# Retention attention and a bilinear feed-forward on one core: other zero products, 64x128 state updates and a new order in the first two pairs

## Chip, cores, metric

One core of one Trainium2 chip. The metric is device time in microseconds (us) of one execution of the program; the times given are medians over several runs.

## The reference

A retention layer (4 batches, 8 heads, 768 steps, head width 64) is followed by a bilinear feed-forward network with 512 inputs and 1536 hidden columns. All inputs and the result are float32.

```python
gamma = 1.0 - 2.0 ** (-5.0 - np.arange(H))
for t in range(S):
    state = gamma * state + einsum('bhd,bhe->bhde', k[:, :, t], v[:, :, t])
    y[:, :, t] = (1 / sqrt(D)) * einsum('bhd,bhde->bhe', q[:, :, t], state)
x = y.transpose(0, 2, 1, 3).reshape(B * S, H * D)      # 3072 x 512
out = ((x @ w_a) * (x @ w_b)) @ w_out                  # 512 -> 1536 -> 512
```

The kernel computes the retention in chunks. With powers of gamma folded into q and k ("scalings", two tables `ktab` and `qtab`), a chunk's result is masked scores times v (within the chunk) plus q times the running state (from the chunks before).

## The kernel before

The 3072 rows are 24 slots of 128 rows. The first six slots (the first batch) are handled as three pairs: a pair is 256 rows, of which slot `par` (0 or 1) holds the even or the odd ones, and a pair has two chunks c of 128 rows each. All other slots take another path (`casts`, `turn`, `scores`, `inter`, `intra`), which the change does not touch. Feed-forward work is cut into eight row tiles J of 512 or 256 rows; tile 0 is the rows of pairs 0 and 1.

Order is written out by hand. Every engine instruction goes through `seq`, which chains it to the one before on its engine, so the order in the source is the order on each engine; semaphores between engines are added by the framework from the tiles that instructions share. There is no planner.

The steps of a pair u, with their names:

- `casts2` (L376) scales k and q into bf16 (`scaled`, L212) and casts v (L184), each on the engine that is named: `D_` is DVE (VectorE), `G_` is POOL (GpSimd), `A_` is ACT (ScalarE).
- `flip2` (L387) transposes k or q on PE (TensorE, L396) into PSUM and copies the result to SBUF (`kT2`, `qT2`).
- `scores2` (L399) makes one slot's scores as 16 products in 64x64 quarters of the PE array (L409); `mask2` (L415) multiplies them with the causal mask on DVE, as two instructions (r = 0, 1).
- `update2` (L422) adds a chunk's k-v products to the state in PSUM (L432), as 16 products in 64x64 quarters; `keep_state` (L439) copies the state's two diagonal halves to `gbd` in SBUF with two ACT instructions.
- `intra2` (L454) multiplies masked scores with v (32 products per pair, L461), `inter2` (L443) adds queries times the kept state (L449). Both write `y`, a PSUM bank for each chunk; `leave2` (L466) copies `y` to `xt`, the input of the feed-forward, one instruction for a chunk.
- `warm` (L481) issues products with a tile of zeros (L484). They compute nothing that is used and keep PE busy.

The state makes pair 0 and pair 1 a chain: an update of chunk c, its copy to `gbd`, the next update into the same bank, and so on; `inter2` of a chunk needs the copy made after the chunk before.

The feed-forward: `ffn_a` (L497) is four products for x @ w_a of 128 hidden columns and an ACT copy of the result, `ffn_g` (L510) four products for x @ w_b and a DVE multiplication with that copy, `ffn_out` (L535) the last product. For tile 0 and the first two groups of hidden columns (ft 0 and 1) the rows are split in two halves: the first half are the rows of pair 0, the second those of pair 1. `parts` (L491) splits the rows for ft 2 and 3 as well, into two products of 256 columns within one instruction group. Pair 2 is worked on between the groups of tile 0.

PSUM has eight banks here: three rotating ones (`psff`, tag "ff"), `y0`, `y1`, the two banks of `at`, and one for the state (`st`).

Loads are DMAs on SyncE's queue in the order of `LOADS`: k and q of pair 0, k and q of pair 1, v of both, and then the weights, which POOL casts to bf16 (`cast_w`, `cast_o`). The first ten are issued at the start. POOL works in the order of the source, too.

Of the kernel before, what the change touches and what calls it, by code (L numbers as in the profile page):

```python
# [9 lines left out]
F32 = mybir.dt.float32  # L10
BF16 = mybir.dt.bfloat16
# [12 lines left out]
def kernel(  # L24
# [10 lines left out]
    nc = tc.nc  # L35
# [86 lines left out]

    kqb = {}
    issue_loads(10)
    zero = const.tile([P, 2 * P], BF16, name="zero")
    seq(nc.vector.memset(zero, 0.0))  # L126
    lgr = const.tile([P, 1, H], F32, name="lgr")
    bq = const.tile([P, 1], F32, name="bq")
# [106 lines left out]
    def half(i):  # L235
        return slice(64 * i, 64 * i + 64)
# [139 lines left out]
    def casts2(u, on):  # L376
        if 2 * u not in kqb:
            for t in (2 * u, 2 * u + 1):
                new_nat(t)
        for (i, par), eng in on.items():  # L380
            t = 2 * u + par
            if i == V:
                cast(eng, vb[t], raws["v", t])
            else:
                scaled(eng, t, i)

    def flip2(u, i, on, banks=None):  # L387
        into = (kT2, qT2)[i]
        if u not in into:
            into[u] = tra.tile([P, 2, HP, P], BF16, tag="kq"[i] + "T2", name="kq"[i] + "T2", bufs=2)  # L390
        for pars, eng in on:
            pool, tag = (psff, "ff") if banks is None else (psat, banks[pars[0]])
            tp = pool.tile([P, 2, HP, P], BF16, tag=tag, name="tp")[:, : len(pars)]
            for m, par in enumerate(pars):
                for hp in range(HP):
                    seq(nc.tensor.transpose(tp[:, m, hp, :], kqb[2 * u + par][:, i, hp, :, :], ident))  # L396
            cast(eng, into[u][:, pars[0] : pars[0] + len(pars)], tp)

    def scores2(u, par, ff=False):  # L399
        t = 2 * u + par  # L400
        if not ff:
            both = psat.tile([P, 2, HP, P], F32, tag="at", name="at")
            at = [both[:, r] for r in range(2)]
        else:
            at = [psff.tile([P, HP, P], F32, tag="ff", name=f"at{r}") for r in range(2)]
        for hp in range(HP):
            for c in range(2):
                for r in range(2):
                    seq(nc.tensor.matmul(at[r][half(c), hp, :],  # L409
                                         kT2[u][half(r), par, hp, half(c)],  # L410
                                         qT2[u][half(r), :, hp, half(c)],
                                         start=True, stop=True, skip_group_check=True))
        ats[t] = at

    def mask2(u, par):  # L415
        t = 2 * u + par
        aT[t] = tra.tile([P, 2, HP, P], BF16, tag="aT", name="aT")
        for r in range(2):
            seq(nc.vector.tensor_tensor(aT[t][:, r], ats[t][r], masks[par].to_broadcast([P, HP, P]),  # L419
                                        op=ALU.mult))  # L420

    def update2(u, c, keep=True):  # L422
        if (u, c) == (PAIRS - 1, 1):
            return
        if (u, c) == (0, 0):
            state[0] = psst.tile([P, HP, D], F32, tag="st", name="st")
        st = state[0]
        for par in range(2):
            for hp in range(HP):
                for r in range(2):  # L430
                    t = 2 * u + par
                    seq(nc.tensor.matmul(st[half(r), hp, :], kb[t][half(c), hp, r, :],  # L432
                                         vb[t][half(c), HP * r + hp, :],
                                         start=((u, c, hp, par) == (0, 0, 0, 0)),
                                         stop=(hp == HP - 1), skip_group_check=True))
        if keep:
            keep_state(c)

    def keep_state(c):  # L439
        for r in range(2):  # L440
            seq(nc.scalar.copy(gbd[1 - c][half(r), :, half(r)], state[0][half(r), :, :]))

    def inter2(u, last=False):  # L443
        for c in range(2):
# [9 lines left out]
    def intra2(u, par, begin, home=(psat, "y0", "y1")):  # L454
        if begin:
            ys[u] = [home[0].tile([P, HP, P], F32, tag=home[1 + c], name="y") for c in range(2)]
        t = 2 * u + par
        for r in range(2):
            for hp in range(HP):
                for c in range(2):  # L460
                    seq(nc.tensor.matmul(ys[u][c][half(hp % 2), 2 * r + hp // 2, :],  # L461
                                         vb[t][half(c), HP * r + hp, :], aT[t][half(c), r, hp, :],
                                         start=(begin and r == 0 and hp < 2), stop=not begin,
                                         skip_group_check=True))
# [11 lines left out]
    def xcols(J, kt, c0, c1):  # L476
        if J < 2:
            return xt[J][:, c0 // P : c1 // P, kt, :]
        return xt[J][:, kt, c0:c1]

    def warm(n, pool, tag, w=2 * P):  # L481
        idle = pool.tile([P, 4 * P], F32, tag=tag, name="idle")
        for _ in range(n):
            seq(nc.tensor.matmul(idle[:, :w], zero[:, :P], zero[:, :w], start=True, stop=True,  # L484
                                 skip_group_check=True))
# [2 lines left out]

    asbs = {}

    def parts(J, ft, c0, c1):  # L491

        if J == 0 and ft in (2, 3):
            return [(c0, (c0 + c1) // 2), ((c0 + c1) // 2, c1)]
        return [(c0, c1)]

    def ffn_a(J, ft, c0=0, c1=None):  # L497
        c1 = TILES[J] * P if c1 is None else c1
        if J not in ht:
            ht[J] = htp.tile([P, NFT, 4 * P], BF16, tag="ht", name="ht")  # L500
        fs = slice(ft * P, (ft + 1) * P)
        a = psff.tile([P, 4 * P], F32, tag="ff", name="a")[:, : c1 - c0]
        for kt in range(KT):
            for b0, b1 in parts(J, ft, c0, c1):
                seq(nc.tensor.matmul(a[:, b0 - c0 : b1 - c0], wa_bf[:, kt, fs], xcols(J, kt, b0, b1),  # L505
                                     start=(kt == 0 and b0 == c0), stop=(kt == KT - 1 and b1 == c1),
                                     skip_group_check=True))
        asb = asbs[J, ft, c0] = asbp.tile([P, 4 * P], BF16, tag="asb", name="asb")[:, : c1 - c0]
        seq(nc.scalar.copy(asb, a))  # L509

    def ffn_g(J, ft, c0=0, c1=None):
        c1 = TILES[J] * P if c1 is None else c1
        fs = slice(ft * P, (ft + 1) * P)
        g = psff.tile([P, 4 * P], F32, tag="ff", name="g")[:, : c1 - c0]
        for kt in range(KT):
            for b0, b1 in parts(J, ft, c0, c1):
                seq(nc.tensor.matmul(g[:, b0 - c0 : b1 - c0], wb_bf[:, kt, fs], xcols(J, kt, b0, b1),  # L517
                                     start=(kt == 0 and b0 == c0), stop=(kt == KT - 1 and b1 == c1),
                                     skip_group_check=True))
# [88 lines left out]
    for ft in range(2, NFT):  # L608
# [9 lines left out]
            ffn_g(0, ft + 1)  # L618
        if ft == 8:
            ffn_ab(0, ft)  # L620
    flip2(2, K, [((0, 1), A_)], ("y0",))
    ffn_a(0, 9)
    flip2(2, Q, [((0,), D_), ((1,), D_)], ("y1", "y0"))
    ffn_g(0, 9)
# [80 lines left out]
```

## Time and profile before

| | |
|---|---|
| median of 3 runs | 226.02 us (225.84 to 283.55) |
| the profiled execution | 226.63 us |
| its span, first to last instruction | 224.9 us |
| PE busy | 218.5 us (97%), 2632 products |
| DVE, ACT, POOL busy | 96.3 us, 96.3 us, 80.4 us |
| moved by DMA | 39.72 MB |

How to read the profile: times are us from the start of the span. PE's products are pipelined, so a product's row lasts longer than the distance to the next one; what a product costs in a stream is the distance between starts. "Timeline" rows give the start, the time to the end of the last of a group, engine, source line, output<-inputs, tile shapes and count; in brackets stands how long the engine was idle before, and who ended it. "Waits" rows give who waited for whom, the total, the count and the longest.

### The profile page before, as it was taken

The numbers are of one execution on the slowest core, as the hardware profiler recorded it, in microseconds if no ns is written. First come the engines' busy times: TensorE is split into PE (matmuls) and PEld (weight loads), VectorE is DVE, ScalarE is ACT, GpSimd is POOL, SyncE is SP. The second block draws the span as 40 slices with busy tenths as digits, with TensorE's granted clock in tenths as the row PEclk, the third lists the DMA queues.
The fourth block names the chain that finished last, engine by engine and source line by source line (L and its number), as shares of the span: only waits on it lengthen the run. The fifth ranks groups of instructions, "written<-read, shape, count | busy, mean of one in ns | idle before, by whom it ended". The sixth has DMA issues, their size and how long they took to land.

```text
span 224.9 us, 6284 instructions
## 1 busy us (share of the span) xinstructions
PE 218.5 (97%) x2632; PEld 133.5 (59%) x2632; DVE 96.3 (43%) x195; ACT 96.3 (43%) x207; POOL 80.4 (36%) x105
## 2 busy tenths in 40 slices
PE   8879999999999999999999999999999999999994
PEld 8768645686456866876875444554444544444443
DVE  3784347553406435472466333544343521334300
ACT  3475435433427426454457333355333354333221
POOL 5577798682544335350533535251000000000000
PEclk9999999999999999999999999999999999999999
DMA  6999999899999994988958899895100012100022
GB/s 179 347 379 383 365 314 407 260 206 194 228 243 271 222 223 80 223 222 186 212 135 194 127 226 239 187 235 146 47 0 0 3 50 93 47 3 1 0 93 95
DMA packets 96124, 39.72 MB, mean 177 GB/s; under 512 B 76000, under 2 KB 91616, under 8 KB 96096
## 3 DMA queue, kind: packets, MB, share of 16 engines
q1 hardware_dynamic: 95952, 39.20, 67.8%
q8 instruction: 20, 0.33, 0.6%
q10 hardware_dynamic: 144, 0.13, 0.2%
q14 instruction: 8, 0.07, 0.1%
HBM read 28.31 MB, written 6.29 MB: 154 GB/s over the span
## 4 chain that ended last, share of the span: by engine, by line
PE 96%; DVE 1%; issue 1%; ACT 0%
PE o L545 28%; PE a L505 28%; PE g L517 28%; PE idle L484 3%; PE y L321 1%; PE at L280 1%; PE y L333 1%; PE tp L396 1%; PE st L257 1%; PE y L449 1%; PE st L432 1%; DVE aT L419 1%; DVE kqb L212 1%; PE y L461 0%; PE at L409 0%
## 5 line engine op out<-in xcount | busy, mean ns | idle before, releaser
L520 DVE TENSOR_TENSOR ht<-g,asb 128x256 bf16<-128x256 f32 (+1 forms) x98 | 53.9, 550 | 84.2 <-PE g L517 74.3
L505 PE MATMUL a<-xt,wa_bf 128*128 128x256 bf16 (+1 forms) x400 | 77.6, 319 | 0.0
L517 PE MATMUL g<-xt,wb_bf 128*128 128x256 bf16 (+1 forms) x400 | 77.6, 319 | 0.0
L509 ACT CAST asb<-a 128x256 bf16<-128x256 f32 (+1 forms) x98 | 46.3, 473 | 71.2 <-PE a L505 71.2
L545 PE MATMUL o<-wo_bf,ht 128*128 128x512 bf16 (+2 forms) x312 | 64.4, 363 | 0.0
L505 PEld LDWEIGHTS <-wa_bf 128*128 128x128 bf16 x400 | 38.8, 98 | 24.0 <-DVE xt L184 0.4
L517 PEld LDWEIGHTS <-wb_bf 128*128 128x128 bf16 x400 | 39.0, 98 | 23.0
L545 PEld LDWEIGHTS <-ht 128*128 128x128 bf16 x312 | 28.8, 98 | 30.5
L212 POOL TENSOR_TENSOR kqb<-kf,ktab 128x512 bf16<-128x512 f32 x22 | 22.9, 1044 | 40.5 <-DMA kf<-in_k_dram 35.9
L182 ACT COPY osb<-o 128x512 f32<-128x512 f32 (+2 forms) x25 | 14.1, 565 | 32.9 <-PE o L545 27.6
L184 POOL CAST vb<-vf 128x512 bf16<-128x512 f32 x25 | 15.0, 613 | 24.0 <-DMA vf<-in_v_dram 21.6
L212 POOL TENSOR_TENSOR kqb<-qf,qtab 128x512 bf16<-128x512 f32 x21 | 22.3, 1066 | 0.0
L182 ACT CAST gst<-sums 128x256 bf16<-128x256 f32 x33 | 13.4, 405 | 6.3 <-DVE sums L271 3.0
L271 DVE TENSOR_TENSOR sums<-st,sums 128x256 f32<-128x256 f32 x30 | 12.7, 424 | 1.9 <-PE st L257 0.3
L286 DVE TENSOR_TENSOR aT<-at,mask 128x512 bf16<-128x512 f32 x18 | 11.5, 680 | 0.0
L484 PE MATMUL idle<-zero 128*128 128x170 bf16 (+1 forms) x56 | 8.1, 321 | 1.1 <-DVE zero L126 1.1
L344 ACT CAST xt<-y 128x512 bf16<-128x512 f32 x16 | 8.5, 584 | 0.0
L419 DVE TENSOR_TENSOR aT<-at,mask 128x512 bf16<-128x512 f32 x12 | 7.5, 681 | 0.4 <-PE at L409 0.4
L484 PEld LDWEIGHTS <-zero 128*128 128x128 bf16 x56 | 6.7, 130 | 1.3 <-DVE zero L126 1.1
L184 POOL CAST wb_bf<-wstb 128x1024 bf16<-128x1024 f32 (+1 forms) x7 | 6.4, 922 | 2.8 <-DMA wstb<-in_moe_w_b_dram 2.8
L184 POOL CAST wo_bf<-wsto 128x1024 bf16<-128x1024 f32 x6 | 6.3, 1043 | 2.8 <-DMA wsto<-in_moe_w_out_dram 2.8
L184 POOL CAST wa_bf<-wsta 128x1024 bf16<-128x1024 f32 (+1 forms) x7 | 6.4, 921 | 1.2 <-DMA wsta<-in_moe_w_a_dram 1.1
(53 smaller groups left out, 87.0 us busy)
## 6 DMA issues: line engine op xcount, KB each, us to landing
out_dram<-osb SPq DMA_DIRECT2D x23, 256.0 KB, 3.1
kf<-in_k_dram SPq DMA_DIRECT2D x18, 256.0 KB, 4.3
qf<-in_q_dram SPq DMA_DIRECT2D x18, 256.0 KB, 4.5
vf<-in_v_dram SPq DMA_DIRECT2D x18, 256.0 KB, 5.2
wsta<-in_moe_w_a_dram SPq DMA_DIRECT2D x6, 512.0 KB, 7.7
wstb<-in_moe_w_b_dram SPq DMA_DIRECT2D x6, 512.0 KB, 7.9
wsto<-in_moe_w_out_dram SPq DMA_DIRECT2D x6, 512.0 KB, 8.2
kf<-in_k_dram SPq DMA_DIRECT2D x3, 512.0 KB, 5.8
```

Source lines behind the costliest of these rows:

```text
L182: seq(nc.scalar.copy(dst, src))
L184: seq(engine.tensor_copy(dst, src))
L212: seq(eng.tensor_tensor(dst, src, tab, op=ALU.mult))
L271: seq(nc.vector.tensor_tensor(new, u[c][:, s], old, op=ALU.add))
L286: seq(nc.vector.tensor_tensor(aT[n][:, r].rearrange("p s h d -> p (s h) d"), at[:, r].rearrange("p s h d -> p (s h) d"), mask.to_broadcast ...
L419: seq(nc.vector.tensor_tensor(aT[t][:, r], ats[t][r], masks[par].to_broadcast([P, HP, P]), op=ALU.mult))
L484: seq(nc.tensor.matmul(idle[:, :w], zero[:, :P], zero[:, :w], start=True, stop=True, skip_group_check=True))
L505: seq(nc.tensor.matmul(a[:, b0 - c0 : b1 - c0], wa_bf[:, kt, fs], xcols(J, kt, b0, b1), start=(kt == 0 and b0 == c0), stop=(kt == KT - 1 a ...
L509: seq(nc.scalar.copy(asb, a))
L517: seq(nc.tensor.matmul(g[:, b0 - c0 : b1 - c0], wb_bf[:, kt, fs], xcols(J, kt, b0, b1), start=(kt == 0 and b0 == c0), stop=(kt == KT - 1 a ...
L520: seq(nc.vector.tensor_tensor(ht[J][:, ft, c0:c1], g, asbs.pop((J, ft, c0)), op=ALU.mult))
L545: seq(nc.tensor.matmul(o, ht[J][:, ft, i * P : (i + 1) * P], wo_bf[:, ft, c0:c1], start=(ft == 0), stop=(ft == NFT - 1)))
```

## The change

Only the first pairs' work, the zero products and tile 0's ft 2 and 3 are touched.

- Zero products: the tile of zeros is widened from 256 to 512 columns. The groups after the first become 8 of 64 columns (were 8 of 256), 2 of 128 (were 4 of 256), 4 of 192 (were 4 of 256), and two groups of 3 of 512 columns into the state's bank, between pair 1's transposes and after them (was one group of 4 of 256).
- `update2`: for each slot and head pair one product with 64 rows and 128 columns instead of two 64x64 quarters. It makes four 64x64 blocks, of which two are used, as before. So 8 products of 128 columns take the place of 16 of 64; this holds for pair 2 also. `keep_state` can put its two copies on two engines, which is used once: ACT and DVE after `update2(1, 0)`.
- Pair 1's k of slot 1 is scaled on DVE (was POOL), its q of slot 1 on DVE between the two masks of slot 0 of pair 0. The second q copy of pair 0 goes from DVE to ACT.
- Pair 1's q transposes use the banks y1 and y0, scores of slot 0 use `at` and those of slot 1 the rotating banks (it was the other way round for both pairs).
- Pair 1's `y` is one tile of two banks under the tag `at` (it was two rotating banks).
- Order: scores of pair 1 stand ahead of the first state update and within pair 0's `intra2`; `intra2` of pair 0 is finished, and its first `y` copied, ahead of the second update; `intra2(1, 0)` stands ahead of `update2(1, 0)`; the first feed-forward group stands ahead of `inter2(1)`.
- `parts` is gone: ft 2 and 3 of tile 0 are single products of 512 columns.

```diff
-    zero = const.tile([P, 2 * P], BF16, name="zero")
+    zero = const.tile([P, 4 * P], BF16, name="zero")
...
     def update2(...):
-        for r in range(2):
-            seq(nc.tensor.matmul(st[half(r), hp, :], kb[t][half(c), hp, r, :],
-                                 vb[t][half(c), HP * r + hp, :], ...
+        seq(nc.tensor.matmul(st[:, hp, :], kb[t][half(c), hp, :, :],
+                             vb[t].rearrange("p (r hp) d -> p hp r d", r=2)[half(c), hp], ...
...
     def keep_state(c, on=(nc.scalar, nc.scalar)):
         for r in range(2):
-            seq(nc.scalar.copy(gbd[1 - c][half(r), :, half(r)], state[0][half(r), :, :]))
+            cast(on[r], gbd[1 - c][half(r), :, half(r)], state[0][half(r), :, half(r)])
...
     def intra2(u, par, begin, home=None):
+            both = psat.tile([P, 2, HP, P], F32, tag=home, name="y")
+            ys[u] = [both[:, c] for c in range(2)]
...
-    casts2(1, {(K, 0): G_, (K, 1): G_, (Q, 0): G_})
+    casts2(1, {(K, 0): G_, (K, 1): D_, (Q, 0): G_})
...
-    warm(8, psat, "y1")
+    warm(8, psat, "y1", 64)
     flip2(0, Q, [((0,), A_)])
-    warm(4, psat, "y1")
-    flip2(0, Q, [((1,), D_)])
-    warm(4, psat, "y1")
-    scores2(0, 0, True)
-    scores2(0, 1)
+    warm(2, psat, "y1", P)
+    flip2(0, Q, [((1,), A_)])
+    warm(4, psat, "y1", 192)
+    scores2(0, 0)
+    scores2(0, 1, True)
+    mask2(0, 0, (0,))
     casts2(1, {(Q, 1): D_})
+    mask2(0, 0, (1,))
+    mask2(0, 1)
     flip2(1, K, [((0, 1), A_)])
-    flip2(1, Q, [((1,), A_), ((0,), A_)])
-    mask2(0, 0)
-    mask2(0, 1)
-    warm(4, psat, "y1")
+    warm(3, psst, "st", 4 * P)
+    flip2(1, Q, [((1,), A_), ((0,), A_)], ("y0", "y1"))
+    warm(3, psst, "st", 4 * P)
+    scores2(1, 0)
     update2(0, 0)
-    scores2(1, 0, True)
+    mask2(1, 0)
     intra2(0, 0, True)
+    scores2(1, 1, True)
+    mask2(1, 1)
     intra2(0, 1, False)
+    leave2(0, (A_, None))
     update2(0, 1)
-    leave2(0, (A_, None))
-    scores2(1, 1)
-    mask2(1, 0)
-    mask2(1, 1)
     inter2(0, True)
     leave2(0, (None, D_))
-    update2(1, 0)
-    intra2(1, 0, True, (psff, "ff", "ff"))
+    intra2(1, 0, True, "at")
+    update2(1, 0, (A_, D_))
     intra2(1, 1, False)
+    W2 = 2 * P
+    ffn_a(0, 0, 0, W2)
     inter2(1, True)
     leave2(1, (A_, D_))
-    W2 = 2 * P
-    ffn_a(0, 0, 0, W2)
-    update2(1, 1, False)
     ffn_a(0, 1, 0, W2)
+    update2(1, 1, None)
     issue_loads(100)
     cast_w(1)
     ffn_g(0, 0, 0, W2)
     ffn_a(0, 0, W2, 2 * W2)
```

The built program of the changed kernel shows two semaphore waits that the diff does not spell out: DVE's half of the state copy after `update2(1, 0)` waits for ACT's half, and DVE's copy of pair 1's second `y` waits for ACT's copy of the first (before, the two `y` copies waited for PE alone). PE has 112 rows fewer (80 from five updates, 32 from ft 2 and 3); SyncE's order is the same, and POOL's only lacks the one scaling.

More of the change, by code (lines that the diff above doesn't have):

```diff
@@ L425, in update2 @@
         if (u, c) == (0, 0):
-            state[0] = psst.tile([P, HP, D], F32, tag="st", name="st")
+            state[0] = psst.tile([P, HP, P], F32, tag="st", name="st")
         st = state[0]
@@ L452, in inter2, with intra2 @@
                                          skip_group_check=True))
-    def intra2(u, par, begin, home=(psat, "y0", "y1")):
-        if begin:
-            ys[u] = [home[0].tile([P, HP, P], F32, tag=home[1 + c], name="y") for c in range(2)]
+    def intra2(u, par, begin, home=None):
+        if begin and home is None:
+            ys[u] = [psat.tile([P, HP, P], F32, tag=f"y{c}", name="y") for c in range(2)]
+        elif begin:
+            both = psat.tile([P, 2, HP, P], F32, tag=home, name="y")
+            ys[u] = [both[:, c] for c in range(2)]
         t = 2 * u + par
@@ L503, in ffn_a @@
         for kt in range(KT):
[L504 to L507, printed above, removed]
+            seq(nc.tensor.matmul(a, wa_bf[:, kt, fs], xcols(J, kt, c0, c1),
+                                 start=(kt == 0), stop=(kt == KT - 1)))
         asb = asbs[J, ft, c0] = asbp.tile([P, 4 * P], BF16, tag="asb", name="asb")[:, : c1 - c0]
@@ L515, in ffn_g @@
         for kt in range(KT):
[L516 to L519, printed above, removed]
+            seq(nc.tensor.matmul(g, wb_bf[:, kt, fs], xcols(J, kt, c0, c1),
+                                 start=(kt == 0), stop=(kt == KT - 1)))
         seq(nc.vector.tensor_tensor(ht[J][:, ft, c0:c1], g, asbs.pop((J, ft, c0)), op=ALU.mult))
```

31 lines of the change are left out of this document (14 added, 17 removed).

## Prediction

> **What bounds the kernel now.** I read the page's first part, then PE's waits, then the timeline of each engine over the head.
>
> ```profile
> PE 218.5 (97%) x2632; PEld 133.5 (59%) x2632; DVE 96.3 (43%) x195; ACT 96.3 (43%) x207; POOL 80.4 (36%) x105
> ```
>
> ```profile
> PE idle L484 <- DVE zero L126: 1.1, 1, 1.1
> PE y L449 <- issue: 0.9, 1, 0.9
> PE tp L396 <- DVE aT L419: 0.7, 2, 0.5
> ```
>
> PE bounds the kernel, and its waits are all in the head: no row names a wait of the feed-forward. So there are two terms only: when the stream of PE that never waits begins, and what PE work is added behind that point. As its start I take the first `a` product on pair 1's rows (19.25 below): the same instructions follow it in both kernels. The timeline of PE up to there:
>
> ```profile
> 9.42 0.64 PE L409 MATMUL at<-qT,kT 64*64 64x128 bf16 x32
> ...
> 12.50 0.44 PE L432 MATMUL st<-vb,kqb 64*64 64x64 bf16 x16
> 12.80 0.42 PE L409 MATMUL at<-qT,kT 64*64 64x128 bf16 x16
> 13.02 0.64 PE L461 MATMUL y<-aT,vb 64*64 64x128 bf16 x32
> 13.79 0.35 PE L432 MATMUL st<-vb,kqb 64*64 64x64 bf16 x11
> ...
> 14.38 0.41 PE L449 MATMUL y<-qT,gbd 128*64 128x128 bf16 x7
> 15.73 0.22 PE L449 MATMUL y<-qT,gbd 128*64 128x128 bf16 x1 [0.94 <-issue]
> 15.87 0.37 PE L432 MATMUL st<-vb,kqb 64*64 64x64 bf16 x12
> ...
> 16.69 0.83 PE L449 MATMUL y<-qT,gbd 128*64 128x128 bf16 x16
> 17.46 0.61 PE L505 MATMUL a<-xt,wa_bf 128*128 128x256 bf16 x4
> 18.00 0.44 PE L432 MATMUL st<-vb,kqb 64*64 64x64 bf16 x16
> 18.37 0.61 PE L505 MATMUL a<-xt,wa_bf 128*128 128x256 bf16 x4
> 18.82 0.60 PE L517 MATMUL g<-xt,wb_bf 128*128 128x256 bf16 x4
> 19.25 1.04 PE L505 MATMUL a<-xt,wa_bf 128*128 128x256 bf16 x8
> ```
>
> The reader sees the chain of the state: update 12.50, update 13.79, update 15.87, and a stall of 0.94 us ahead of the third, on the last product of a group that was already running. "Issue" means that no semaphore explains it. One more row bears on it, from the DMA view of 13.2 to 13.3 us:
>
> ```profile
> q8 instruction: 1, 0.02, 54.9%
> ```
>
> A packet of instructions starts to arrive some 1.5 us ahead of the stall. I read the stall as PE waiting for its own next block of instructions. The stalled product is instruction 450 of PE's built program.
>
> **The change part by part.** The prices: four products of 256 columns take 19.25 - 18.82 = 0.43, so 0.109 each. Sixteen quarter updates take 18.37 - 18.00 = 0.37 with the change to full-array products; 0.1 of that is the change, since 17.46 to 18.00 is 0.54 for four products of 0.109. So a quarter update group costs 0.27. The new one is eight products of 128 columns on the same 64 rows. No row shows this form. Below, it goes at the pace of L449's products on half of the columns, two side by side: row 14.38 has seven in 0.41, and one lasts 0.22 (row 15.73), so (0.41 - 0.22) / 6 = 0.03 each and 0.25 a group. Above, 128 columns one after another cost half of 256, 0.055 each, 0.45 a group. I take 0.45, since the new products use all columns and cannot run side by side. Results land about 0.2 after a product's start (0.22 for one, row 15.73).
>
> The other engines' rows in the head:
>
> ```profile
> 6.34 1.29 DVE L212 TENSOR_TENSOR kqb<-qf,qtab 128x512 bf16<-128x512 f32 x2 [0.18 <-DMA qf<-in_q_dram]
> 8.94 0.42 DVE L184 COPY qT<-tp 128x512 bf16<-128x512 bf16 x1 [1.30 <-PE tp L396]
> 9.33 1.17 DVE L212 TENSOR_TENSOR kqb<-qf,qtab 128x512 bf16<-128x512 f32 x1
> 10.42 2.47 DVE L419 TENSOR_TENSOR aT<-at,mask 128x512 bf16<-128x512 f32 x4
> ```
>
> ```profile
> 7.90 2.04 POOL L212 TENSOR_TENSOR kqb<-kf,ktab 128x512 bf16<-128x512 f32 x2 [3.64 <-DMA kf<-in_k_dram]
> 9.91 1.49 POOL L212 TENSOR_TENSOR kqb<-qf,qtab 128x512 bf16<-128x512 f32 x1
> ```
>
> ```profile
> 6.87 1.07 ACT L182 COPY kT<-tp 128x512 bf16<-128x512 bf16 x2 [1.86 <-PE tp L396]
> ...
> 11.57 1.18 ACT L182 COPY qT<-tp 128x512 bf16<-128x512 bf16 x2
> 12.98 0.76 ACT L441 CAST gbd<-st 64x256 bf16<-64x256 f32 x2 [0.22 <-PE st L432]
> ...
> 15.03 0.73 ACT L182 CAST xt<-y 128x512 bf16<-128x512 f32 x1
> ```
>
> 1. Fewer zero products and ACT for both q copies. ACT's k copies end at 7.94; two more copies follow at once (1.07 for two) and end at 8.95. Scores start at 9.0 (0.06 from DVE's copy to PE in the rows 8.94 and 9.42), 0.4 earlier. The wider tile of zeros only delays the first zero products, which end before anything that counts; if not, 0.1.
>
> 2. Scalings of pair 1. DVE's scaling took 1.17 where two alone took 1.29, and POOL's 1.49 where two took 2.04: where the two engines scale at once, one waits for the other. Now both start when k lands (7.90): DVE 7.8 to 8.5, POOL behind it to 9.4, as late as scores end. POOL's q follows, 9.35 to 10.4. DVE masks at 9.45, then its q scaling waits for POOL's and ends at 10.95. Pair 1's q transposes run at 11.0, ACT copies 11.4 to 12.5 (before 12.75). Gain so far 0.25. The seven other mask instructions, 0.6 each, run without a break to 15.5, ahead of who needs them. The two groups of three 512-column zero products (0.65 each) lie in the waits for DVE and ACT (10.0 to 10.65 and 11.45 to 12.1) and cost nothing; without that cover they would cost 1.3.
>
> 3. Scores of pair 1 now stand ahead of the first update: scores 12.55, update 12.85 (before 12.50), landed 13.45. Copies 0.76 on ACT, to 14.25; second update at 14.3 (before 13.79), landed 14.9. Meanwhile `intra2` and the other scores (0.2 a group of 16) fill PE. ACT now copies `y` (0.73, from 14.35) ahead of the state: the copies run 15.1 to 15.85, and the third update starts at 15.9, where before it started at 15.87. `inter2(0)` runs at 14.85 and `intra2(1, 0)` at 15.2. Instruction 450 now is a product at the end of `intra2(1, 0)`, at 15.4. If its block lands at 15.73 as before, the stall ends before the update is free: what the stall cost is not gained, a wait for ACT takes its place.
>
> 4. From there PE is full: update 15.9 to 16.35, `intra2(1, 1)` to 16.7, `a` 16.8 to 17.25, `inter2(1)` 17.35 to 17.8, landed 18.0. The state copies of ACT and DVE, one behind the other, end at 17.35 and are just in time. Then `a` 17.9, update 18.45, `g` 19.0 to 19.45.
>
> 5. The copies of pair 1's `y` are now serial. Before, ACT and DVE overlapped:
>
> ```profile
> 17.20 0.74 ACT L182 CAST xt<-y 128x512 bf16<-128x512 f32 x1
> ```
>
> ```profile
> 17.57 0.73 DVE L184 CAST xt<-y 128x512 bf16<-128x512 f32 x1 [0.85 <-PE y L449]
> ```
>
> Now ACT 18.05 to 18.75, DVE 18.8 to 19.55, and the next `a` waits for DVE: 19.6 instead of 19.25. **Loss 0.35.** Without this wait PE would be there at 19.45.
>
> 6. Behind the head: the update of pair 2, in the dense stream, costs 0.45 instead of 0.27: **loss 0.2** (0 with the cheap form). `parts`: 16 products of 0.109 against the 512-column pace, eight in 26.66 - 24.93 = 1.73; **gain 0.03** over both tiles.
>
> ```profile
> 24.93 1.89 PE L505 MATMUL a<-xt,wa_bf 128*128 128x512 bf16 x8
> 26.66 1.89 PE L517 MATMUL g<-xt,wb_bf 128*128 128x512 bf16 x8
> ```
>
> Sum: 0.35 + 0.2 - 0.03 = 0.5 later. The profiled execution took 226.63 (span 224.9 and 1.7 around it), and would take 227.1; it lay 0.6 above the median of 226.02. I put the sum on the median: **226.5 us**.
>
> **The rivals.**
>
> A. *The cheap update.* At 0.25 a group `intra2(0, 1)` and ACT's `y` copy behind it come 0.2 earlier, so does the third update, and it ends 0.2 sooner again: `inter2(1)` lands at 17.6, and `a` starts at 19.2; pair 2 costs nothing more. 0.1 earlier: 225.9. For it speaks that PE overlaps small products wherever rows show quarters; against, that the new form has one row half and all columns.
>
> B. *The serial copies do not bind* and updates are cheap: `a` follows `g`, at 19.45 less 0.4 and less 0.2 for the update between, 18.85, which is 0.4 earlier: 225.6. Against it: the built program has the wait.
>
> C. *The stall is not instructions.* Then it belongs to the last product of `inter2(0)`, goes where that goes, and holds it from 15.05 to 16.05; `intra2(1, 0)` and the third update follow at 16.45, all of point 4 and 5 is 0.55 later: 227.1. The Trainium skill (Runtime: NRT & Kernel Launch, section "Instruction fetch mechanics") says that instructions come in blocks of 256 and that crossing a block is mostly hidden; by "mostly hidden" this rival would gain, by the trace's 0.94 us right behind a packet the fetch is the better reading.
>
> D. *The clock falls*, because the early zero products are fewer. PE's products ran at half pace in the first microseconds:
>
> ```profile
> 1.12 5.28 PE L484 MATMUL idle<-zero 128*128 128x170 bf16 x36 [1.12 <-DVE zero L126]
> ```
>
> That is 0.14 for 170 columns, against 0.109 for 256 later. A fall that lasts as long as this stretch, 5.3 us, costs half of it in the dense stream: 226.5 + 2.6 = 229.1. Two falls, 231.8, which is over 2% slower; that is the point from which this rival decides. Against it:
>
> ```profile
> 7.00:10.40 3.40, 3.32 (x67) 2.78 (x64) 2.10 (x4) 1.52 (x3) 2.50 (x3) 1.00 1.15 346
> 10.40:13.80 3.40, 2.53 (x82) 2.02 (x80) 3.03 (x6) 2.83 (x5) 3.23 (x5) 1.00 1.12 372
> 13.80:17.20 3.40, 2.46 (x100) 1.83 (x99) 2.72 (x5) 2.20 (x6) 1.92 (x4) 1.00 1.08 379
> ```
>
> PE was busy 98%, 74% and 72% of these stretches (2nd column by the first), and the clock (1.00) held. In the changed kernel the longest idle time I find is 0.6 (8.4 to 9.0), and the first stretch has some 2.8 of 3.4 busy. The Trainium skill (TensorE: Matmul & The Clock Gate, section "Part 1: The HAM clock gate") lets the clock fall after an idle window of about 3.4 us; by that rule it does not fall here at all.
>
> **How the numbers follow.** Forecast 0.55 (226.2 to 226.9); A 0.2; B 0.1; C 0.1; D 0.05. The likeliest gives 226.5. The range takes in A, B and C with 0.3 to 0.4 above C for a late block and for array changes: 225.4 to 227.5, and leaves D out. Over 2% (4.5 us; about what a measurement of this kernel can tell from no change) is out of reach on the fast side: all PE waits of the head together are 2.7, so 0.01. Slower by over 2% is D's double fall and what I have not seen: 0.04. Within 2%: 0.95.
>
> **What would show it.** Right: scores at 9.0; third update near 15.9 behind an ACT state copy; eight updates in 0.45; pair 1's second `y` copy on DVE starting as ACT's ends; `a` on pair 1's rows at 19.6 with a wait for DVE of 0.15; no wait of PE later. Wrong: an "issue" wait of PE after 15.9 (C), a granted clock under 1.00 behind 7 us (D), eight updates in 0.25 (A), `a` before 19.2 (B). A wait inside the feed-forward would make the two-term view itself wrong.

## The result, and the profile after

| | before | after |
|---|---|---|
| median, same chip | 225.93 us | 227.23 us (226.89 to 227.48) |
| ratio | | 1.0062, 95% interval 1.0041 to 1.0083 |
| the profiled execution, its span | 226.63 us, 224.9 us | 227.30 us, 225.6 us |
| PE products | 2632 | 2576 |

One of the four runs of the kernel before took 283.55 us; the ratio leaves it out. The change costs 0.9 to 1.9 us. The forecast was 0.5 us and no difference over 2%; the time lies within its range, near the upper end.

The first part of the page after, the row of PE:

```profile
PE 217.3 (96%) x2556; PEld 130.9 (58%) x2576; DVE 97.0 (43%) x196; ACT 96.3 (43%) x207; POOL 79.7 (35%) x104
```

PE holds 2556 rows of products for 2576 weight loads: 20 records are missing. Keep that in mind for the waits of PE (total, count, longest):

```profile
PE idle L488 <- DVE zero L126: 1.3, 1, 1.3
PE o L539 <- issue: 1.1, 7, 0.2
PE tp L396 <- DVE kqb L212: 0.9, 3, 0.4
PE at L409 <- ACT qT L182: 0.6, 2, 0.3
PE y L321 <- issue: 0.2, 1, 0.2
```

The second row, seven gaps of at most 0.2 inside the steady stream, is where records are missing; the weight loads run through. The last row is a real stall, found below. The 0.94 of "issue" that the kernel before had on `inter2` is gone. The timeline of PE over the head:

```profile
8.92 0.64 PE L409 MATMUL at<-qT,kT 64*64 64x128 bf16 x32 [0.34 <-ACT qT L182]
...
11.25 0.62 PE L396 MATMUL tp<-ident,kqb 128*128 128x128 bf16 x8 [0.41 <-DVE kqb L212]
...
12.80 0.42 PE L409 MATMUL at<-qT,kT 64*64 64x128 bf16 x16 [0.29 <-ACT qT L182]
13.15 0.62 PE L432 MATMUL st<-vb,kqb 64*128 64x128 bf16 x8
13.70 0.42 PE L465 MATMUL y<-aT,vb 64*64 64x128 bf16 x16
...
16.05 0.60 PE L432 MATMUL st<-vb,kqb 64*128 64x128 bf16 x8
16.59 0.42 PE L465 MATMUL y<-aT,vb 64*64 64x128 bf16 x16
16.94 0.61 PE L502 MATMUL a<-xt,wa_bf 128*128 128x256 bf16 x4
17.48 0.64 PE L450 MATMUL y<-qT,gbd 128*64 128x128 bf16 x16
18.05 0.61 PE L502 MATMUL a<-xt,wa_bf 128*128 128x256 bf16 x4
18.59 0.62 PE L432 MATMUL st<-vb,kqb 64*128 64x128 bf16 x8
19.14 0.61 PE L512 MATMUL g<-xt,wb_bf 128*128 128x256 bf16 x4
19.72 1.03 PE L502 MATMUL a<-xt,wa_bf 128*128 128x256 bf16 x8
```

The reader sees a head in which PE hardly waits after 12.80 and is still later at the end: `a` on pair 1's rows starts at 19.72, before at 19.25. Two short waits have no bracket in this view: the third update (16.05) starts 0.36 behind the product ahead of it, where a change of form without a wait takes 0.15, and the last `a` waits 0.13 for DVE. An update takes 0.53 to 0.55 from its start to the next group's.

The other engines' rows that the prediction spoke of, DVE, POOL and ACT after:

```profile
7.92 0.69 DVE L212 TENSOR_TENSOR kqb<-kf,ktab 128x512 bf16<-128x512 f32 x1
...
10.00 1.19 DVE L212 TENSOR_TENSOR kqb<-qf,qtab 128x512 bf16<-128x512 f32 x1
...
18.93 0.74 DVE L184 CAST xt<-y 128x512 bf16<-128x512 f32 x1 [1.35 <-ACT xt L182]
```

```profile
8.04 1.47 POOL L212 TENSOR_TENSOR kqb<-kf,ktab 128x512 bf16<-128x512 f32 x1 [3.81 <-DMA kf<-in_k_dram]
9.60 1.04 POOL L212 TENSOR_TENSOR kqb<-qf,qtab 128x512 bf16<-128x512 f32 x1
```

```profile
11.68 1.07 ACT L182 COPY qT<-tp 128x512 bf16<-128x512 bf16 x2 [0.44 <-PE tp L396]
...
15.26 0.74 ACT L182 CAST gbd<-st 64x256 bf16<-64x256 f32 x2
...
18.16 0.74 ACT L182 CAST xt<-y 128x512 bf16<-128x512 f32 x1 [0.20 <-PE y L450]
```

ACT's state copies end at 16.00 (15.26 and 0.74), and the third update starts 0.05 behind them: that is what it waited for.

**Behind the head** two more things cost. Pair 2's group of scores, update and first `a`, after, and then in a second profile of the kernel before (span 224.4):

```profile
36.87 0.64 PE L409 MATMUL at<-qT,kT 64*64 64x128 bf16 x32
37.45 0.62 PE L432 MATMUL st<-vb,kqb 64*128 64x128 bf16 x8
38.00 0.39 PE L502 MATMUL a<-xt,wa_bf 128*128 128x512 bf16 x1
```

```profile
36.18 0.64 PE L409 MATMUL at<-qT,kT 64*64 64x128 bf16 x32
36.65 0.42 PE L432 MATMUL st<-vb,kqb 64*64 64x64 bf16 x16
37.11 0.38 PE L505 MATMUL a<-xt,wa_bf 128*128 128x512 bf16 x1
```

From scores to `a` it is 1.13 after and 0.93 before: 0.20 more. And at 121 us, timeline of PE after, one product of a group stands apart from the other fifteen:

```profile
120.61 0.21 PE L321 MATMUL y<-kqT,gst 64*64 64x64 bf16 x1
121.02 0.31 PE L321 MATMUL y<-kqT,gst 64*64 64x64 bf16 x15 [0.20 <-issue]
```

From 120.61 to 121.02 nothing starts (the bracket counts idle time only, after the first product's 0.21). No semaphore explains it: the same picture as before's stall at L449, in another place. The DMA view of 118.7 to 118.8 holds a packet of instructions:

```profile
q8 instruction: 1, 0.02, 60.1%
```

### The profile page after: what moved, and what is told of

It reads as the page before. It is cut to its first block, busy times and chain, and to the rows that moved or that the text cites. A ratio compares the mean times of both kernels' runs of the same rounds, so it can differ in the third digit from the quotient of the medians.

```text
span 225.6 us, 6154 instructions
## 1 busy us (share of the span) xinstructions
PE 217.3 (96%) x2556; PEld 130.9 (58%) x2576; DVE 97.0 (43%) x196; ACT 96.3 (43%) x207; POOL 79.7 (35%) x104
## 4 chain that ended last, share of the span: by engine, by line
PE 92%; DMA 2%; ACT 2%; issue 1%; DVE 1%; SPq 0%; DVEq 0%
PE a L502 28%; PE g L512 28%; PE o L539 27%; DMA qf<-in_q_dram 2%; PE y L321 2%; PE at L280 1%; PE y L333 1%; PE st L257 1%; ACT qT L182 1%; PE st L432 1%; PE tp L396 1%; DVE kqb L212 1%; PE at L409 1%; PE y L465 1%; PE y L450 1%
## 5 line engine op out<-in xcount | busy, mean ns | idle before, releaser
L539 PE MATMUL o<-wo_bf,ht 128*128 128x512 bf16 (+2 forms) x299 | 62.5, 362 | 1.4 <-issue 1.1
L502 PEld LDWEIGHTS <-wa_bf 128*128 128x128 bf16 x392 | 38.0, 98 | 25.0 <-DVE xt L184 0.4
L512 PEld LDWEIGHTS <-wb_bf 128*128 128x128 bf16 x392 | 38.1, 98 | 23.8
L212 POOL TENSOR_TENSOR kqb<-kf,ktab 128x512 bf16<-128x512 f32 x21 | 22.3, 1062 | 41.6 <-DMA kf<-in_k_dram 41.6
L212 POOL TENSOR_TENSOR kqb<-qf,qtab 128x512 bf16<-128x512 f32 x21 | 21.8, 1042 | 0.9 <-DMA qf<-in_q_dram 0.7
L488 PE MATMUL idle<-zero 128*128 128x170 bf16 (+4 forms) x55 | 7.0, 291 | 1.3 <-DVE zero L126 1.3
L298 DVE COPY lgr<-bq 128x1 f32<-128x1 f32 x4 | 0.6, 154 | 14.2 <-PE y L321 14.2
```

Of the source, the lines that this page charges most:

```text
L212: seq(eng.tensor_tensor(dst, src, tab, op=ALU.mult))
L502: seq(nc.tensor.matmul(a, wa_bf[:, kt, fs], xcols(J, kt, c0, c1), start=(kt == 0), stop=(kt == KT - 1)))
L512: seq(nc.tensor.matmul(g, wb_bf[:, kt, fs], xcols(J, kt, c0, c1), start=(kt == 0), stop=(kt == KT - 1)))
L539: seq(nc.tensor.matmul(o, ht[J][:, ft, i * P : (i + 1) * P], wo_bf[:, ft, c0:c1], start=(ft == 0), stop=(ft == NFT - 1)))
```

## The experiments

Ratios are to the kernel before on the same chip, with 95% intervals. "`a`" is the first `a` product on pair 1's rows.

### The kernel before, twice more

No edit.

> The kernel before, unchanged. Its profiled execution was 0.6 us above its median. Theory 1 (the stall at instruction 450 comes in every execution): the profile again shows PE waiting for no semaphore at about 15.7, for 0.5 us or more, and the first `a` product on pair 1's rows at 19.1 to 19.3. Theory 2 (it depends on when the block's packet lands, which changes between executions): the stall is gone or shorter, that `a` starts at 18.3 to 18.9, and the span is 0.3 to 0.9 shorter than 224.9. Then the median of the kernel before stands for executions without the stall. The ratio is 1.000 either way.

> The kernel before, unchanged, a third profile. Theory (the stall in the head comes in every execution, of 0.6 to 0.9): `a` on pair 1's rows at 18.9 to 19.3 with PE waiting for no semaphore at 15.4 to 15.8. Rival (now and then): no such wait and `a` at 18.3 to 18.6. The ratio is 1.000 either way.

Measured: 226.01 us, ratio 1.0007 [0.9992, 1.0022], and 225.97 us, 0.9998 [0.9982, 1.0013]; the spans of both profiles are 224.4. PE's timeline in the one and the other:

```profile
15.46 0.22 PE L449 MATMUL y<-qT,gbd 128*64 128x128 bf16 x1 [0.65 <-issue]
15.61 0.37 PE L432 MATMUL st<-vb,kqb 64*64 64x64 bf16 x12
...
18.99 1.04 PE L505 MATMUL a<-xt,wa_bf 128*128 128x256 bf16 x8
```

```profile
15.47 0.22 PE L449 MATMUL y<-qT,gbd 128*64 128x128 bf16 x1 [0.65 <-issue]
...
19.00 1.04 PE L505 MATMUL a<-xt,wa_bf 128*128 128x256 bf16 x8
```

The stall comes in all three profiles, 0.94, 0.65 and 0.65. The one that the prediction was made on had the longest: its `a` at 19.25 is 0.25 later than in the others, and its span 0.5 longer. The kernel before is better read as `a` at 19.0 and span 224.4. When the head begins also differs a little from one execution to the next, in both kernels. So where one profile is compared with another below, part of a difference in `a` can stand at pair 1's scores already.

### Quarter updates in the changed kernel

```diff
-                seq(nc.tensor.matmul(st[:, hp, :], kb[t][half(c), hp, :, :],
-                                     vb[t].rearrange("p (r hp) d -> p hp r d", r=2)[half(c), hp], ...
+                for r in range(2):
+                    seq(nc.tensor.matmul(st[half(r), hp, half(r)], kb[t][half(c), hp, r, :],
+                                         vb[t][half(c), HP * r + hp, :], ...
```

> The changed kernel, with update2 again as 16 products in 64x64 quarters. Theory (the wide updates and the serial copies make the loss): an update group takes 0.3 us of PE instead of the 0.54 seen in the changed kernel's trace; the first a product on pair 1's rows comes 0.4 earlier than its 19.7 and pair 2's update is 0.25 cheaper, together 0.65 us less: ratio to before about 1.003. Rival (the loss lies outside the updates, in new instruction-block stalls or the start): no change, ratio 1.006.

Measured: 226.42 us, ratio 1.0015 [1.0001, 1.0029]; span 224.5. `a` in PE's timeline:

```profile
19.07 1.03 PE L503 MATMUL a<-xt,wa_bf 128*128 128x256 bf16 x8
```

That is 0.65 earlier than in the changed kernel. Of this 0.14 stands at pair 1's scores already (12.66 against 12.80), ahead of every update, so the quarters are worth 0.51 there. With 0.20 for pair 2's update that is 0.7. The wide updates carry most of the loss. The ratio fell somewhat further than expected (1.0015, not 1.003); the quarters also add 80 rows to PE's program, which matters below.

### Pair 1's second y in a bank of its own

```diff
-            both = psat.tile([P, 2, HP, P], F32, tag=home, name="y")
-            ys[u] = [both[:, c] for c in range(2)]
+            ys[u] = [psat.tile([P, 2, HP, P], F32, tag=home, name="y")[:, 0],
+                     psat.tile([P, HP, P], F32, tag="y0", name="y")]
```

> The changed kernel, with pair 1's second y in the bank y0 instead of the second bank of the tile at, so that DVE's copy of it waits for PE and no longer for ACT's copy. Theory: DVE's copy starts at about 18.15 instead of 18.9, the a product on pair 1's rows follows g without a wait, 0.15 us earlier: ratio about 1.005. Rival (the serial copies are most of the head's loss): 0.4 earlier or more, ratio 1.004.

Measured: 227.09 us, ratio 1.0050 [1.0032, 1.0069]; span 225.2.

```profile
19.42 0.82 PE L502 MATMUL a<-xt,wa_bf 128*128 128x256 bf16 x6
```

`a` follows `g` (18.97) without a wait. It is 0.30 earlier than after, of which 0.17 was there at the update before it already (18.42 against 18.59): the wait itself is worth 0.13 in this kernel. The ratio is as expected, but the time is not told apart from that of the changed kernel.

### Both

Both diffs above.

> The changed kernel with quarter updates and with pair 1's second y in a bank of its own, so that its two copies overlap. Theory (the two steps 5 and 6 of the prediction are the cost, and they add): the wide updates cost 1.0015 against 1.0062 of the whole, the serial copies 0.0012, so the ratio to the kernel before is about 1.000 (225.9 to 226.3 us); `a` on pair 1's rows starts at about 18.9 without a wait for DVE, against 19.07 with the quarters alone. Rival (what is left of the loss is not in these two but in the order of the head): `a` starts at 19.0 or later and the ratio stays at 1.002 or above.

Measured: 226.18 us, ratio 1.0009 [0.9994, 1.0024].

```profile
18.73 1.04 PE L503 MATMUL a<-xt,wa_bf 128*128 128x256 bf16 x8
```

With quarters the wait was worth 0.34 (19.07 to 18.73), since `g` ends earlier; 0.03 of it stands at pair 1's scores already. With both parts undone the rest of the change, its new order included, is level with the kernel before: the loss goes with these two parts. `a` is 0.26 earlier than before's 18.99 and the kernel is not faster: PE stood at 119.6 us for 0.43 (start to start, the place discussed below).

### Wide updates in the kernel before

```diff
-            state[0] = psst.tile([P, HP, D], F32, tag="st", name="st")
+            state[0] = psst.tile([P, HP, P], F32, tag="st", name="st")
...
-                for r in range(2):
-                    seq(nc.tensor.matmul(st[half(r), hp, :], kb[t][half(c), hp, r, :], ...
+                seq(nc.tensor.matmul(st[:, hp, :], kb[t][half(c), hp, :, :],
+                                     vb[t].rearrange("p (r hp) d -> p hp r d", r=2)[half(c), hp], ...
```

> The kernel before, with update2 as 8 products of 64 rows and 128 columns; nothing else is changed. Each update costs 0.2 to 0.25 more. PE has 32 rows fewer ahead of the third update. Theory (the stall before the third update is PE waiting for its next block of instructions, whose border stays at instruction 450): the stall leaves the last product of inter2(0), the third update starts 0.3 to 0.4 earlier than 15.87, and the sum is only 0.2 slower: ratio 1.001. Rival (the stall belongs to that product): it stays there, and the sum is three updates in the head and one in the stream, 0.6 to 0.85 slower: ratio 1.003 to 1.004.

Measured: 226.64 us, ratio 1.0027 [1.0011, 1.0043]; span 225.2. PE's timeline, and its waits:

```profile
15.38 0.62 PE L431 MATMUL st<-vb,kqb 64*128 64x128 bf16 x8
...
19.12 1.04 PE L504 MATMUL a<-xt,wa_bf 128*128 128x256 bf16 x8
```

```profile
PE at L280 <- issue: 0.4, 1, 0.4
```

The third update starts 0.23 earlier than before's 15.61, since no stall is left in `inter2(0)`; the slower updates eat that, `a` is 0.13 later. A new stall stands at 120 us. So the time agrees nearly with the rival's figure, but not for its reason: the stall did not stay in `inter2(0)`. (The copy to `gbd`, not shown in the cut, reads the matching half of the wider bank.)

### More rows ahead of everything, in the kernel before

```diff
-    warm(36, psat, "y1", 170)
+    warm(52, psat, "y1", 118)
```

> The kernel before, with the first zero products as 52 of 118 columns instead of 36 of 170: the same columns, 32 more PE rows ahead of everything. Theory (instruction block): the issue wait moves to instruction 450, which is now among the scores of pair 1's second slot, and the last product of inter2(0) has none of its own; time as before within 0.3 us. Rival: the issue wait stays on the last product of inter2(0).

Measured: 228.62 us, ratio 1.0126 [1.0085, 1.0167]; its profiled execution took 230.35. The expectation missed: the stall did not come at the scores. PE's waits, its `a`, and the stretch of 101.8 to 105.2 us (its length, busy time and count of PE, PEld, DVE, ACT and POOL, then the granted clock, DMA's share and GB/s):

```profile
PE y L333 <- issue: 2.2, 1, 2.2
...
PE o L545 <- issue: 0.4, 1, 0.4
```

```profile
18.59 0.82 PE L505 MATMUL a<-xt,wa_bf 128*128 128x256 bf16 x6
```

```profile
101.80:105.20 3.40, 3.40 (x10) 1.19 (x9) 0.00 (x0) 0.01 (x1) 0.03 (x1) 0.53 1.21 301
```

The head has no stall any more, and `a` comes at 18.59, 0.40 earlier than in the kernel before. But 80 us later, where nothing was changed, PE stands for 2.2 us on L333, then runs a stretch at a clock of 0.53 (about 1.6 of 3.4 us lost), and stands once more at 126 us. The slow clock did not come in every run: the two longest of the six (230.35 and 230.61 us) have a mean granted clock of 0.991 and 0.984, the other four (227.91 to 228.69) 0.999 or 1.000.

Counted in PE's built program, weight loads included, the products that stood still are just behind row 450 (before), 3266 (after, and with wide updates at 120 us), 2754 and 3522 (this run). These are 450 + 256 x 0, 11, 9 and 12 (one row more or less). The page counts 20 packets of q8 with 0.33 MB, 16.5 KB each. So PE's program comes in blocks of 256 rows, and PE stood where a block was late. In these stalls PE goes on 1.3 to 1.6 us behind the end of the block's packet: 14.12 to 15.73 (before), 14.21 to 15.46 (second profile), 119.73 to 121.02 (after), 99.65 to 100.97 (this run).

The traces bear this out further. In the 13 profiles without missing records PE crosses 247 such borders. With the n-th packet taken for the n-th border, no crossing comes sooner than 1.25 us behind the end of its packet, and at every border where PE stood for 0.27 us or more, start to start, and no semaphore explains it, it went on 1.25 to 1.61 behind it. Some crossings within these bounds show no stand: there the block was just in time.

### Step 1 alone

```diff
-    warm(8, psat, "y1")
+    warm(8, psat, "y1", 64)
     flip2(0, Q, [((0,), A_)])
-    warm(4, psat, "y1")
-    flip2(0, Q, [((1,), D_)])
-    warm(4, psat, "y1")
+    warm(4, psat, "y1", 64)
+    flip2(0, Q, [((1,), A_)])
+    warm(4, psat, "y1", 192)
```

> The kernel before with step 1 alone: narrow zero products (8 of 64, 4 of 64, 4 of 192, as many as before, so that every later PE instruction keeps its number) and both q copies of pair 0 on ACT. Theory (PE's stall in the head is a late instruction block, and the block is asked for when PE comes to a certain instruction): scores start at 9.0 instead of 9.42, the block is asked for 0.4 earlier, the stall of 0.94 shrinks by 0.3 or more or is gone, and the kernel takes 0.3 to 0.7 us less than before: ratio 0.997 to 0.999. Rival 1 (the block's time is fixed from the start of the program): PE goes on at 15.73 as before, and the ratio is 1.000. Rival 2 (DVE and POOL scalings of pair 1 set the head): scores at 9.0, but pair 1's q transposes at 11.15 as before, ratio 1.000.

Measured: 225.96 us, ratio 1.0004 [0.9990, 1.0019]; span 224.3.

```profile
15.16 0.38 PE L432 MATMUL st<-vb,kqb 64*64 64x64 bf16 x12 [0.26 <-ACT gbd L441]
...
18.57 1.04 PE L505 MATMUL a<-xt,wa_bf 128*128 128x256 bf16 x8
```

PE's row numbers are those of before; against the second profile of before PE comes to row 194 (256 ahead of the border) at 9.34 instead of 9.91, the packet starts at 11.82 instead of 13.25, and the stall is gone, a wait of 0.26 for ACT stands there. The stall fits the theory and not the first rival. The time missed the theory: the ratio, and pair 1's q transposes (11.25 and 11.85), are as the second rival has them. The last product ends 0.39 earlier (220.85 against 221.24), but the span is only 0.16 shorter. At the end of the program DVE's closing drain starts 0.4 later than those of SP and ACT (223.93 against 223.54); in the kernel before they come together. DVE has one instruction fewer here. Why its drain is late was not tried.

### Wide zero products in the changed kernel

```diff
-    warm(8, psat, "y1", 64)
+    warm(8, psat, "y1")
     flip2(0, Q, [((0,), A_)])
-    warm(2, psat, "y1", P)
+    warm(2, psat, "y1", 4 * P)
     flip2(0, Q, [((1,), A_)])
-    warm(4, psat, "y1", 192)
+    warm(4, psat, "y1")
```

> The changed kernel with as many zero products as it has, but as wide as before in the first three groups (8 of 256, 2 of 512, 4 of 256). Theory (pair 1's scalings set the head of the changed kernel, step 2): scores of pair 0 start 0.3 to 0.5 later, pair 1's q transposes stay at 11.2 or are later by at most 0.2, and the time is that of the changed kernel within 0.2 us: ratio to the kernel before 1.006 to 1.007. Rival (the early scores are worth their 0.4): `a` on pair 1's rows comes 0.4 later, at 20.1, ratio 1.008.

Measured: 226.97 us, ratio 1.0049 [1.0031, 1.0067], not told apart from the changed kernel.

```profile
8.93 0.64 PE L409 MATMUL at<-qT,kT 64*64 64x128 bf16 x32 [0.24 <-ACT qT L182]
```

Its `a`:

```profile
19.47 1.03 PE L502 MATMUL a<-xt,wa_bf 128*128 128x256 bf16 x8
```

The time is as the theory has it, but for another reason: the scores are not later (8.93 against 8.92), and `a` is 0.25 earlier, not later. So the narrower zero products bought nothing that can be seen. That ACT's copies of both q tiles brought the scores forward is likely, but not shown: the start of the scores moves by a few tenths between executions (8.72 in the second profile of the changed kernel, 9.03 in the kernel before with more rows, which has neither). The 0.25 of `a` stands at pair 1's scores already (12.55 against 12.80), where POOL's scaling had started 0.22 earlier.

### Step 1 with four PE rows fewer

```diff
-    warm(36, psat, "y1", 170)
+    warm(34, psat, "y1", 180)
```

(on top of step 1 alone.)

> The kernel before with step 1 (as in the run before with step 1 alone) and with the first zero products made 34 of 180 columns instead of 36 of 170: the same columns, four PE rows fewer, so that every later border of 256 rows comes four rows later in the program. With step 1 alone PE stood 0.33 us at row 2754 of its program (101.5 us), where the 256 rows up to it pass in 4.06 us; four rows on they take 4.5. Theory (a border costs what its block comes late, so the rows around it decide): that stall is gone or under 0.1, a new one of up to 0.2 may come at row 2242 (84 us), `a` on pair 1's rows stays at 18.6, and the time is 0.2 to 0.4 below step 1 alone: ratio to the kernel before 0.9985 to 0.9995, the fastest so far. Rival (the loss behind the head belongs to that place and not to a border): the stall stays at 101.5 us, ratio 1.000.

Measured: 226.07 us, ratio 1.0006 [0.9994, 1.0017]. `a` at 18.43, and no standing at row 2754 (step 1 alone had 0.34 there, start to start, where 0.22 is the normal distance); but 0.44 start to start at row 3266 (119 us), where step 1 alone had 0.14. DVE's closing drain is late here too (224.00, SP's 223.61). The forecast of the stall held and that of the time did not: one border was cured, a later one was lost. No version here beats the kernel before.

### Forty PE rows fewer in the changed kernel

```diff
-    warm(36, psat, "y1", 170)
+    warm(16, psat, "y1", 382)
```

> The changed kernel with its first zero products made 16 of 382 columns instead of 36 of 170 (6112 columns instead of 6120): 40 PE rows fewer, nothing else. The border at row 3778 of PE's program then lies behind a stretch whose 256 rows pass in 2.95 us, at 146 us, where nothing waits in the changed kernel. In the traces so far a block's packet starts 0.9 to 2.1 us after PE is 256 rows ahead of it, takes 0.9 to 1.2, and PE goes on 1.3 to 1.5 behind its end. Theory (borders): a new stall of 0.3 to 1.8 us at 146 us on row 3778, the one at 121 us stays at about 0.4, the head as in the changed kernel (`a` on pair 1's rows at 19.6 to 19.8): 0.3 to 1.8 us above the changed kernel, ratio to the kernel before 1.008 to 1.014. Rival (the stall at 121 us belongs to its place, and the count of rows is of no account): no wait at 146 us, the time of the changed kernel, ratio 1.006.

Measured: 227.16 us, ratio 1.0049 [1.0032, 1.0067].

```profile
120.59 0.23 PE L333 MATMUL y<-aT,vb 64*64 64x64 bf16 x5
121.50 0.41 PE L333 MATMUL y<-aT,vb 64*64 64x64 bf16 x27 [0.68 <-issue]
```

The expectation missed in its main point: no wait at 146 us. The packet for row 3778 started under 0.4 us behind PE's passing 256 rows ahead of it, not 0.9 to 2.1, and was there in time. What did come: the stall at 121 us moved to another instruction, 40 rows later in the stream and again on row 3266 of the program, so it belongs to the count and not to L321. In the run with pair 1's second `y` in a bank of its own, which has the rows of the changed kernel, PE does not stand there at all. Where a block can be late follows from the count; whether it is, and by how much, only the run tells.

### The changed kernel again

> The changed kernel, unchanged. Theory (the stall at row 3266 comes in most executions of this program): PE stands 0.3 to 0.6 us at 120.5 to 121.1 us for no semaphore, `a` on pair 1's rows starts at 19.6 to 19.8, the span is 225.3 to 225.8. Rival (it comes now and then): no stall there, span 225.0 to 225.2, and the median of the changed kernel is made by executions without it.

Measured: 227.29 us, ratio 1.0042 [1.0024, 1.0059]; `a` at 19.70, span 225.9.

```profile
120.54 0.20 PE L321 MATMUL y<-kqT,gst 64*64 64x64 bf16 x1
121.30 0.32 PE L321 MATMUL y<-kqT,gst 64*64 64x64 bf16 x15 [0.56 <-issue]
```

The stall at row 3266 is there again, 0.76 start to start instead of 0.41, and the span is 0.3 longer by it.

## Why the prediction was right or wrong

The sign, the class and the range were right, the size was not: 0.5 forecast, 1.3 between the medians. Against the second profile of before the profile after adds up: `a` 0.73 later (18.99 to 19.72), pair 2's update 0.20, less 0.04 up to there for `parts`, and 0.34 behind that, where the stall at row 3266 lies (0.41 start to start), together 1.23; the last products are 1.22 apart, the spans 1.2.

**Step 1** was right in its time (9.0, measured 8.92). Of its two causes the narrower zero products did nothing that shows, as wide ones had the scores at 8.93; that ACT's copies did it is not shown by itself. The wider tile of zeros starts the first zero products at 1.25 instead of 1.12; PE then waits for DVE's scaling, so nothing came of it.

**Step 2** had the mechanism and was up to 0.25 short. DVE's scaling took 1.19 and POOL's 1.47, one behind the other, as foreseen. The Trainium skill (SBUF — State Buffer, section "Who interferes with whom") has DVE instructions with two SBUF inputs and POOL instructions that read SBUF shut each other out; the rows agree. But POOL started later (8.04, where 7.90 was taken) and its q scaling ended at 10.64 instead of 10.4, pair 1's q transposes ran at 11.25 instead of 11.0, and ACT's copies ended at 12.75, as before: the gain of 0.25 put down there is not in this profile. It comes and goes with the start of the scalings: in the seven profiles with this head pair 1's scores start at 12.55 to 12.80, and at 12.55, as forecast, in the one with wide zero products.

**Step 3** failed in the price of the wide update. 0.45 a group was taken; the eight products start 0.055 apart, 0.44 in all, as the upper bound had it, but a change of tiling stands on each side. The scores' last product and the update's first are 0.15 apart and so are the update's last and the next group's first, where the update's own products go every 0.055. So a group costs about 0.65 between quarters (7 x 0.055 and the two gaps, less one normal distance), while sixteen quarters, which need no change there, take 0.30 (12.50 to 12.80 in the prediction's rows). The Trainium skill (TensorEngine Tiling (Array Packing), section "Key Properties") says that changing the tiling mode drains the engine; the two gaps of 0.15 agree.

The third update came at 16.05 (15.9 forecast), right behind ACT's state copies (to 16.00). So what the stall had cost was not gained, and a wait for ACT took its place, as forecast; the longer updates are in it, since ACT's first state copy starts 0.66 behind the start of a wide update (13.15 to 13.81) and 0.48 behind one in quarters (12.50 to 12.98 in the prediction's rows).

**Step 4** held in its distances: from the third update to `g` it is 3.09 (3.1 forecast), all 0.15 late.

**Step 5** was right: DVE's copy starts where ACT's ends (18.93), `a` waits for it and comes at 19.72 (19.6 forecast). Its worth in the sum was mis-sized. It was counted as 0.35, the distance to the `a` of one profile with a long stall; undoing it alone gives 0.13 of wait and leaves the rest, since slow updates would hold `a` at 19.6 anyway.

**Step 6** was right: 0.20 for pair 2's update, 0.04 for `parts` (0.03 forecast).

**The sum** failed where it was put on the median. It was made against a profiled execution whose stall was 0.29 longer than in the other two profiles, while the changed kernel has no such stall. A difference to an execution that is slow for a cause of its own may not be added to the median: the head loses 0.47 against the first profile and 0.73 against the others. The forecast of 19.6 for `a` itself was good: the four profiles with the changed kernel's head (two of the kernel itself, wide zero products, forty rows fewer) have 19.72, 19.70, 19.47 and 19.59. What was wrong is the 19.25 that it was set against; the other two profiles of the kernel before have 19.0. And the statement that there is no wait of PE later did not look at the next borders, though the stall had been read as an instruction block: row 3266 costs the changed kernel 0.41 and 0.76 in its two profiles, the kernel before 0.27 in one and next to nothing in two.

**Rivals.** A fell: the wide update is dearer than forecast, not cheaper. B fell: the copies bind, by 0.13. C fell: with the row count moved, or with PE at the block earlier, the stall left `inter2(0)`; a wait of PE for "issue" behind 15.9, which the prediction named as C's sign, did come, but at the next late block. The Trainium skill (Runtime: NRT & Kernel Launch, section "Instruction fetch mechanics") calls the crossing of a block mostly hidden; most of the crossings here are, and those that were not cost up to 2.4 us, start to start. D did not come about: the granted clock was 1.00 behind the head.

**Open:** what starts a packet, and so how much of a stall each execution has: in the 13 profiles it starts between 4.0 us ahead of and 4.0 us behind PE's passing 256 rows before the border, in the head 1.5 to 3.5 behind. Also why DVE's drain is late in the two runs with step 1 alone.

## What to carry to other kernels

Before a small product form is traded for a wider one, count what the array changes on both sides cost: 16 quarter products in a stretch of quarters were half the price of 8 wide ones. A stall that no semaphore explains should be counted in rows of the built program; if it recurs at a step of 256, every row that is added or removed ahead moves all later stalls, and a gain in one place can come back as a loss 100 us on. Make the sum against several profiles of the same kernel, not one.

## What the hardware showed that was not expected

- PE crossed no border of 256 program rows sooner than 1.25 us behind the end of the block's packet, in 247 crossings, and the stands at borders ended 1.25 to 1.61 us behind it. They showed where rows pass fast, in the head and in the stretches of 64-wide products: 2.2 us at 99 us with 32 rows more, 0.41 and 0.76 at 121 us in the changed kernel.
- A stall of 2.2 us was followed by a stretch of 3.4 us at a granted clock of 0.53, so it cost about 1.6 us more than itself in that run. The Trainium skill (TensorE: Matmul & The Clock Gate, section "Part 1: The HAM clock gate") lets the clock fall after an idle window of about 3.4 us; here 2.2 us of standing were enough.
- A change from 64x64 to 64x128 tiles and back costs about 0.1 us each way over the normal distance of products (0.15 against 0.05).
